# Attention's results stored in the projection's order from GpSimd's queue, and one block's mean and scale turned by TensorE

## The chip, the cores and the metric

The program runs on one core of a Trainium2 chip. The core has TensorE (PE in the profile: it multiplies matrices; PEld is its loading of weights), VectorE (DVE), ScalarE (ACT), GpSimd (POOL) and SyncE (SP), and 16 DMA engines that all queues share. Each engine works through its own instructions in order and waits for others through semaphores. A DMA is issued by an engine, in that engine's order, and lands later. The metric is device microseconds of one execution.

## The reference

A layer norm without weights, then two branches that read it, and their sum with the input:

```
xn  = layernorm(x)                       # x: 2048 rows of 576, fp32
qkv = xn @ wqkv                          # 32 heads of 18
out = x + attention(q, k, v) @ wo        # each row sees 8 keys: itself and every 2nd row behind it
        + relu(xn @ w1 + b1)**2 @ w2 + b2   # 576 -> 4608 -> 576
```

All is fp32.

## The kernel before

**Tiling.** The 2048 rows are 4 blocks b of 512, the heads 4 groups g of 8. The TensorE operands are split into a high and a low part in fp32r (ACT makes the high part by a copy, DVE the low part by a subtraction), and each product is made from high*high, high*low and low*high. Block 0 is normalised row by row and turned by TensorE (`open_rows`). Blocks 1 to 3 are loaded already turned (`load_xt`, features on the partitions), so mean and inverse standard deviation must lie along the free axis there: `statistics` computes them with rows on the partitions, a small tile `mr` of 128 x 8, line 146 stores it transposed into DRAM (`mr` too), and `load_mb` (line 161) loads it from there to all 128 partitions (`mb`). `normalize` needs `mb`.

**Attention.** `qkv_row` makes k, v and q of 128 rows (line 295), ACT puts them into the stage tile `st` (line 285), and line 288 stores them into DRAM (`kscr`, `vscr`, `qscr`). `fetch` loads them back per (b, g) with the rows behind (lines 315 and 317: `q`, and `kv` for k and for v; 3 `kv` buffers, 2 `q` buffers), so that DVE can work with 4 consecutive rows on each partition (`attention`, lines 333 to 371). The result replaces q and is stored whole by line 369 into DRAM (`o`, 512 rows of 144). The output projection wants other cuts of it: `regroup` (line 661) loads each block back in two parts, columns 0 to 95 into `st` (k = 0) and 96 to 143 into an `r4` buffer (k = 1), with 16 DMAs each (line 671), and DVE, ACT and DVE turn and split the five pieces (`o_hi`, `o_lo`; lines 683 and 684).

**Stages.** `open_rows`, then `q0` (the projection rows of blocks 0 and 1: `row(r)` for r = 0 to 27, with other work between them as `pieces` and attention's steps as `side`), `phase_a(0)` (the first layer of the FFN for blocks 0 and 1 in 18 pairs of feature tiles, with seven products in place of eight, and the second layer for block 0; block 1's activations `h` go to DRAM, line 539), `phase_b0` (the second layer of block 1 from the stored `h`, loaded by line 740, and the projection rows of blocks 2 and 3), `phase_a(1)` and `phase_b1` (the same for blocks 2 and 3). The output projection of a block (`o_ops`) comes at the end of its second layer.

**Order.** It is written out by hand for TensorE, ACT, DVE and SP, in the order in which the Python calls stand (`manual_schedule`). SP issues nearly all DMAs, in that order: if one waits for its data or its buffer, all behind it wait too, among them `w2r` (the second layer's weights, line 444, 3 buffers ahead), `w1r` (the first layer's, line 417) and `h`. GpSimd makes the power for the inverse standard deviation (line 129) and little else.

Of the kernel before, what the change touches and what calls it, by code (L numbers as in the profile page):

```python
# [25 lines left out]
G = 4  # L26
# [19 lines left out]
def block_kernel(ctx: ExitStack, tc: tile.TileContext, x, xt, wqkv, wo, w1, b1, w2, b2, out):  # L46
# [4 lines left out]
    ps = ctx.enter_context(tc.tile_pool(name="ps", bufs=1, space=bass.MemoryType.PSUM))  # L51
    dram = ctx.enter_context(tc.tile_pool(name="dram", bufs=1, space=bass.MemoryType.DRAM))

    ctx.enter_context(tc.manual_schedule(engines={ET.PE, ET.Activation, ET.DVE, ET.SP}))

    xv = x.rearrange("(b p j) d -> b p j d", p=P, j=NJ)
    ov = out[:DM].rearrange("(c p) (b t) -> b p c t", p=P, b=NB)
# [20 lines left out]
    b2t = const.tile([P, 64], F32, name="b2t")[:, :NC]  # L78

    scr = {k: [dram.tile([PAD + S, CG], F32, name=f"{k}scr{g}") for g in range(G)] for k in "kvq"}  # L80
    oscr = {(b, g): dram.tile([TB, CG], F32, name=f"o{b}{g}") for b in range(NB) for g in range(G)}
    mrscr = {b: dram.tile([2 * NJ, P], F32, name=f"mr{b}") for b in range(1, NB)}
    hscr = [[dram.tile([P, 4 * TB], F32, name=f"h{s}{p}") for p in range(NP)] for s in range(2)]

# [52 lines left out]
    def statistics(b):  # L137
        mr = sb.tile([P, 2, NJ], F32, name="mr")
        for j in range(NJ):
            for k in range(2):  # L140
                bn_stats(b, rows_of[b], j, k)
            mean_var(b, j)
            nc.vector.tensor_copy(mr[:, 0, j:j + 1], ln[b, j][:, 0:1])
            inverse_std(mr[:, 1, j:j + 1], ln[b, j][:, 1:2])
            if j == NJ - 1:
                nc.sync.dma_start(mrscr[b].rearrange("n p -> p n"), mr.rearrange("p k j -> p (k j)"))
                measured.add(b)
                release()
            yield

    def load_xt(b):
        xm[b] = sb.tile([P, NC - 1, TB], F32, name="w1r", bufs=2)
        nc.sync.dma_start(xm[b], xt[b, :, :NC - 1])
        xf[b] = {1: lambda: sb.tile([P, DE], F32, name="w2r", bufs=3)[:, :TB],
                 2: lambda: sb.tile([P, TB], F32, name="xf"), 3: lambda: four()[:, 0]}[b]()
        nc.sync.dma_start(xf[b], xt[b, :, NC - 1])

    def load_mb(b):
        assert b in measured
# [139 lines left out]
        a = t[:, j:j + 1, 0:1]  # L299
        return bass.AP(tensor=a.tensor, offset=a.offset, ap=[a.ap[0], [DIL * CG, W], *dims])  # L300

    loads, landed, queue, free = [], {}, [], [0]

    def fetch():
        while free[0] and loads:
            free[0] -= 1
            kind, b, g = loads.pop(0)
            if kind == "x":
                load_rows(b)
                landed["x", b] = True  # L310
                continue
            t = landed[kind, b, g] = sb.tile([P, NE, CG], F32, name="kv", bufs=3)
            if kind == "k":
                q = landed["q", b, g] = sb.tile([P, NJ, CG], F32, name="q", bufs=2)
                nc.sync.dma_start(q.rearrange("p j c -> p (j c)"),
                                  flat(scr["q"][g], (PAD + b * TB) * CG, [NJ * CG, P], NJ * CG))
            nc.sync.dma_start(t.rearrange("p e c -> p (e c)"),
                              flat(scr[kind][g], (PAD + b * TB - HALO) * CG, [NJ * CG, P], NE * CG))

    def release():  # L320
# [12 lines left out]
    def attention(b, g):  # L333
        k, q = landed.pop(("k", b, g)), landed.pop(("q", b, g))
        lg = sb.tile([P, NA, W], F32, name="lg")
        mx = sb.tile([P, NA], F32, name="mx")
        sm = sb.tile([P, NA], F32, name="sm")
        for j in range(NJ):
            pr = sb.tile([P, W, CG], F32, name="pr")
            tt(pr, q[:, j:j + 1].to_broadcast([P, W, CG]), shifted(k, j, [1, CG]), ALU.mult)  # L340
            if j == NJ - 1:
                release()
            yield
            nc.vector.tensor_reduce(out=lg[:, j * HG:(j + 1) * HG].rearrange("p a w -> p w a"),  # L344
                                    in_=pr.rearrange("p w (a d) -> p w a d", d=DH), axis=AX.X, op=ALU.add)
# [12 lines left out]
        v = landed.pop(("v", b, g))  # L358
        for j in range(NJ):
            pr = sb.tile([P, W, CG], F32, name="pr")  # L360
            at = lg[:, j * HG:(j + 1) * HG].rearrange("p a w -> p w a")
            tt(pr.rearrange("p w (a d) -> p w a d", d=DH), at[:, :, :, None].to_broadcast([P, W, HG, DH]),
               shifted(v, j, [DH, HG], [1, DH]), ALU.mult)
            yield
            tt(pr[:, :4], pr[:, :4], pr[:, 4:], ALU.add)
            tt(pr[:, :2], pr[:, :2], pr[:, 2:4], ALU.add)
            tt(q[:, j], pr[:, 0], pr[:, 1], ALU.add)
            if j == NJ - 1:
                nc.sync.dma_start(oscr[b, g].rearrange("(p j) c -> p j c", j=NJ), q)
                release()  # L370
            yield

# [240 lines left out]
    def phase_a(s, filler):  # L613
        b = 2 * s
        ffn_pair(s, 0, filler, first=True)
        open_y(b)
        for p in range(1, NP):
            h, ops = hs.pop(s * NP + p - 1), []

            def work(i):  # L620
                if i in (0, 2):
                    ops.extend(tile_products(b, 2 * p - 2 + i // 2, h))
                add(b, ops[7 * i:7 * i + 7])

# [24 lines left out]
        w2_lo()  # L649
        load_h(s, 2)  # L650
        o_hi(b, 4)
        o_lo(b, 4)
        for c in range(NC):
            w2_hi()
            add(b, o_ops(b, c), range(NC) if c == NC - 1 else ())
            w2_lo()
        finish(b)

    ob = {}

    def regroup(b, k):
        if k == 0:
            t = sb.tile([P, NJ * G, OA], F32, name="st")
        else:
            t = sb.tile([P, NJ * G, OB], F32, name="r4", bufs=4)
        ob[b, k] = t
        a, z = ((0, OA), (OA, CG))[k]
        for g in range(G):
            rows = oscr[b, g].rearrange("(i l j) c -> i l j c", i=G, j=NJ)
            for i in range(G):  # L670
                nc.sync.dma_start(t[g * L:(g + 1) * L].rearrange("l (j i) c -> l i j c", i=G)[:, i],  # L671
                                  rows[i, :, :, a:z])

    ot, of = {}, {}

# [379 lines left out]

    def q0():
        todo = [(b, g, j) for b, g in ((0, 1), (0, 3), (0, 2), (1, 3), (1, 2), (1, 1), (1, 0)) for j in range(NJ)]
        pieces = [statistics(1), once(load_mb, 1), split_wq(3, "S", lambda: load_wq(2)), normalize(1)]

        held = []  # L1060

        def row(r):
# [4 lines left out]
            if j == NJ - 1:  # L1067
# [2 lines left out]
                    if not b and g > 1:  # L1070
                        offer({3: 2, 2: 3}[g])

                if r < 5:
                    held.append(go)
                else:
                    go()

        for r in range(len(todo) - 2):
            row(r)
            if r == 5:  # L1080
                offer(0, 0)
                for late in held:
                    late()
                held.clear()
                pieces.insert(0, split_wq(2, "h", lambda: load_wq(0)))
            if r == 8:
                load_w1(0)
            if r == 11:
                run_all(pieces)
            if r == 15:  # L1090
# [1 line left out]
            if r == 19:  # L1092
                split_up.discard(0)
                pieces.insert(0, split_wq(0, "h"))
            if r == 23:
                run_all(pieces)
                combine_w1(0)
                load_w1(1)
                for n in range(3):
                    load_w2(n)  # L1100
            if r in (24, 25):
                w1_hi(0, r - 24)
                w1_lo(0, r - 24)
            else:
                run(pieces, 3 if r < 4 or 15 <= r < 20 else 2)

        def filler(i):
            if i < 2:
# [11 lines left out]
    nc.sync.dma_start(b1t, b1)  # L1120
    nc.sync.dma_start(b2t, b2)
    load_xt(1)
    with tc.manual_schedule(engines={ET.Pool}):
        open_rows()
    for g in range(1, G):
        for k in "kv":
            nc.sync.dma_start(scr[k][g][:PAD], zero)
# [57 lines left out]
```

## Time and profile before

| | us |
|---|---|
| median of 3 runs (lowest, highest) | 1218.41 (1218.04, 1218.84) |
| profiled execution, its own time | 1218.07 |
| its span | 1216.4 |
| PE busy | 1140.7 |
| DVE busy | 916.5 |
| ACT busy | 573.3 |
| POOL busy | 13.5 |

The span lacks 1.7 us of the execution's own time. PE's busy time leaves 75.7 us of the span; where these lie, and what ends them, is what the prediction reads. The stages in the span: `open_rows` to about 21 us, `q0` to 118, `phase_a(0)` to 477, `phase_b0` to 707, `phase_a(1)` to 1060, `phase_b1` to the end. In the rows shown, a line of the timeline is: start, duration, engine, line, operation, out<-in, count, and in brackets the engine's idle time before it and what ended that; "SPq" is SP issuing a DMA. A line of the waits is: who, for whom, total us, times, longest.

### The profile page before, as it was taken

What the parts mean: (1) busy time and instruction counts of PE and PEld (TensorE: products, weight loads), DVE (VectorE), ACT (ScalarE), POOL (GpSimd) and SP (SyncE); (2) the same over time, 40 slices, a digit from 0 to 9 for tenths busy, and PEclk for the clock granted to TensorE, in tenths of its full rate; (3) what the DMA queues carried; (4) which work ended last, traced back from release to release, by engine and by line L of the source; (5) the groups of instructions that cost most, each with busy time, mean ns of one, the idle gap of its engine ahead of it and who ended that gap; (6) DMA issues with size and microseconds to landing.
All of it is one profiled execution on the core that took longest, in us unless ns stands there. A gap on an engine that the chain in (4) does not pass through costs nothing.

```text
span 1216.4 us, 13713 instructions
## 1 busy us (share of the span) xinstructions
PE 1140.7 (94%) x5013; PEld 950.8 (78%) x5013; DVE 916.5 (75%) x1202; ACT 573.3 (47%) x800; POOL 13.5 (1%) x32
## 2 busy tenths in 40 slices
PE   9695999999999988999999699999999999799968
PEld 7694788888888876888888578888888888578747
DVE  6498588887887855888777577888878787499624
ACT  5323666666676642522232246766666675222121
POOL 3000000000000000000000000000000000000000
PEclk9898999999999998999999899999999999899979
DMA  7575437466466477988766575364545528678573
GB/s 257 178 252 187 160 122 256 147 150 241 156 143 255 121 262 255 348 281 308 268 221 203 142 236 200 107 233 156 200 161 197 202 91 274 229 277 311 200 263 111
DMA packets 107140, 254.25 MB, mean 209 GB/s; under 512 B 30016, under 2 KB 57408, under 8 KB 92480
## 3 DMA queue, kind: packets, MB, share of 16 engines
q1 hardware_dynamic: 106784, 253.00, 61.8%
q8 instruction: 39, 0.64, 0.2%
q10 hardware_dynamic: 288, 0.37, 0.1%
q14 instruction: 29, 0.24, 0.1%
HBM read 191.90 MB, written 61.43 MB: 208 GB/s over the span
## 4 chain that ended last, share of the span: by engine, by line
PE 75%; DMA 8%; DVE 8%; SPq 5%; issue 2%; ACT 2%; POOL 0%; DVEq 0%; ACTq 0%; POOLq 0%
PE p L481 31%; PE p L512 26%; PE p L295 12%; PE p L516 5%; SPq L671 4%; DMA h<-h 3%; DVE pr L93 3%; DVE w2s L93 2%; DMA w2r<-in_wo 1%; DMA w2r<-in_w 1%; DMA mr<-mr 1%; DMA qscr<-st 1%; ACT w2s L454 1%; PE p L973 1%; DVE w1r L93 1%
## 5 line engine op out<-in xcount | busy, mean ns | idle before, releaser
L481 PE MATMUL p<-h,w2s 128*128 128x512 f32 x2010 | 492.1, 393 | 16.7 <-DMA h<-h 13.6
L481 PEld LDWEIGHTS p<-h,w2s 128*128 128x128 f32 x2010 | 378.8, 189 | 102.3 <-issue 14.3
L512 PE MATMUL p<-X,w1s 128*128 128x512 f32 x864 | 221.4, 392 | 13.5 <-ACT w1s L427 11.8
L512 PEld LDWEIGHTS p<-X,w1s 128*128 128x128 f32 x864 | 162.5, 189 | 49.3 <-ACT w1s L427 12.2
L93 DVE TENSOR_TENSOR w2s<-w2r,w2s 128x576 fp32r<-128x576 f32 x164 | 123.4, 754 | 87.9 <-ACT w2s L454 86.4
L454 ACT ACTIVATE w2s<-w2r 128x640 fp32r<-128x640 f32 x164 | 119.8, 732 | 138.1 <-DMA w2r<-in_w 72.0
L512 PE MATMUL p<-S,w1s 128*128 128x512 f32 x648 | 165.5, 391 | 1.8 <-DVE r L93 1.8
L512 PEld LDWEIGHTS p<-S,w1s 128*128 128x128 f32 x648 | 122.1, 189 | 28.1 <-DVE r L93 2.7
L93 DVE TENSOR_TENSOR h<-r,h 128x1024 fp32r<-128x1024 f32 (+2 forms) x78 | 93.2, 1199 | 46.1 <-ACT r L527 45.4
L93 DVE TENSOR_TENSOR w1s<-w1r,w1s 128x1024 fp32r<-128x1024 f32 x72 | 88.2, 1225 | 28.7 <-ACT w1s L427 27.8
L519 ACT ACTIVATE r<-r,b1t 128x512 f32<-128x512 f32 x72 | 51.9, 721 | 116.7 <-DVE r L93 116.7
L285 ACT ACTIVATE st<-p 128x432 f32<-128x432 f32 x64 | 32.9, 528 | 156.7 <-PE p L295 92.4
L481 PE MATMUL p<-w1s,w2s 128*128 128x512 f32 x260 | 73.9, 450 | 27.4 <-ACT w2s L454 27.4
L93 DVE TENSOR_TENSOR pr<-q,kv 128x1152 f32<-128x1152 f32 x64 | 86.7, 1354 | 6.3 <-issue 5.5
L481 PEld LDWEIGHTS p<-w1s,w2s 128*128 128x128 f32 x260 | 57.7, 224 | 43.0 <-ACT w2s L454 29.8
L344 DVE TENSOR_REDUCE lg<-pr 128x64 f32<-128x1152 f32 x64 | 86.5, 1352 | 1.5
L93 DVE TENSOR_TENSOR pr<-lg,kv 128x1152 f32<-128x1152 f32 x64 | 86.7, 1354 | 1.0
L523 ACT ACTIVATE h<-r 128x1024 fp32r<-128x1024 f32 x72 | 76.1, 1057 | 9.2 <-DMA h<-h 8.1
L93 DVE TENSOR_TENSOR pr<-pr 128x576 f32<-128x576 f32 (+1 forms) x128 | 77.6, 607 | 3.4
L427 ACT ACTIVATE w1s<-w1r 128x1024 fp32r<-128x1024 f32 x72 | 75.7, 1051 | 2.0 <-PE p L481 1.9
L527 ACT ACTIVATE r<-r 128x1024 f32<-128x1024 f32 x72 | 76.0, 1055 | 1.2
L516 PE MATMUL p<-x,w1s 128*128 128x512 f32 x216 | 66.5, 389 | 0.0
(124 smaller groups left out, 964.5 us busy)
## 6 DMA issues: line engine op xcount, KB each, us to landing
h<-h SPq DMA_DIRECT2D x72, 1024.0 KB, 5.9
w2r<-in_w SPq DMA_DIRECT2D x144, 320.0 KB, 4.7
w1r<-in_w SPq DMA_DIRECT2D x36, 640.0 KB, 4.0
kv<-kscr SPq DMA_DIRECT2D x16, 1296.0 KB, 7.4
kv<-vscr SPq DMA_DIRECT2D x16, 1296.0 KB, 7.7
r<-in_wqkv SPq DMA_DIRECT2D x16, 432.0 KB, 6.2
w2r<-in_wo SPq DMA_DIRECT2D x20, 320.0 KB, 5.7
w1r<-in_xt SPq DMA_DIRECT2D x6, 1024.0 KB, 6.5
```

The lines of the kernel that those rows point to most:

```text
L93: return nc.vector.tensor_tensor(out=out, in0=a, in1=b, op=op)
L295: nc.tensor.matmul(p[:, :QW], l, r, start=k == 0, stop=k == len(mm) - 1)
L344: nc.vector.tensor_reduce(out=lg[:, j * HG:(j + 1) * HG].rearrange("p a w -> p w a"), in_=pr.rearrange("p w (a d) -> p w a d", d=DH), axis ...
L427: nc.scalar.activation(w1s[n, k][:, 0], raw1[n][:, 4 * k:4 * k + 4], AF.Copy)
L454: nc.scalar.activation(w2s[stream[i]][:, :DE], raw2[i], AF.Copy)
L481: nc.tensor.matmul(yp[b][c], v, a, start=c not in yb[b], stop=c in last and c not in [o[0] for o in ops[i + 1:]], skip_group_check=True)
L512: nc.tensor.matmul(to, l, r, start=start and i == 0, stop=i == len(mm) - 1, skip_group_check=True)
L516: nc.tensor.matmul(to, weight(LEFT, k, f), v, start=False, stop=k == 1, skip_group_check=True)
L519: nc.scalar.activation(to, a, AF.Relu, bias=b1t[:, f:f + 1])
L523: nc.scalar.activation(h[:, 0], r, AF.Square)
L527: nc.scalar.activation(r, r, AF.Square)
L671: nc.sync.dma_start(t[g * L:(g + 1) * L].rearrange("l (j i) c -> l i j c", i=G)[:, i], rows[i, :, :, a:z])
```

## The change

- `attention` stores its result from GpSimd's queue, cut into the projection's two parts and already in the projection's row order: 8 DMAs per (b, g) (4 per part) where there was one on SP. `regroup` is then one plain DMA per part, on GpSimd's queue too, in place of 16 on SP.
- From row 6 of `q0` on, the loads of q, k and v go through GpSimd's queue (`lane`). Those of (0, 0) and the q and k of (0, 1) stay on SP.
- Block 1's `mr` is turned by TensorE into PSUM, copied by ACT to an 8 x 128 tile, and stored by a plain DMA. Blocks 2 and 3 keep the transposing store.
- In `q0` the pieces stand in another order: the statistics and the splitting of group 3's weights are run to the end right behind row 2, and `load_mb(1)`, `load_wq(2)` and the first attention loads are issued there; `load_w1(0)` comes at row 5 (it was row 8), `load_w2` at row 21 (it was row 23).
- At the end of `phase_a`, the third load of `h` is issued behind the second output projection piece, not ahead of the first.
- GpSimd's instructions are now in hand-written order throughout.

```diff
-    ctx.enter_context(tc.manual_schedule(engines={ET.PE, ET.Activation, ET.DVE, ET.SP}))
+    ctx.enter_context(tc.manual_schedule(engines={ET.PE, ET.Activation, ET.DVE, ET.SP, ET.Pool}))
...
-    oscr = {(b, g): dram.tile([TB, CG], F32, name=f"o{b}{g}") for b in range(NB) for g in range(G)}
+    OPART = ((0, OA), (OA, CG))
+    oscr = {(b, k): dram.tile([P, NJ * G, z - a], F32, name=f"o{b}{k}") for b in range(NB) for k, (a, z) in enumerate(OPART)}
...
-                nc.sync.dma_start(mrscr[b].rearrange("n p -> p n"), mr.rearrange("p k j -> p (k j)"))
+                if b > 1:
+                    nc.sync.dma_start(mrscr[b].rearrange("n p -> p n"), mr.rearrange("p k j -> p (k j)"))
+                mrs[b] = mr
...
+    def turn_mr(b, i):
+        y = bank(i)
+        nc.tensor.transpose(y[:2 * NJ, :P], mrs[b].rearrange("p k j -> p (k j)"), ident)
+        t = sb.tile([2 * NJ, P], F32, name="mrt")
+        nc.scalar.activation(t, y[:2 * NJ, :P], AF.Copy)
+        nc.sync.dma_start(mrscr[b], t)
...
-                nc.sync.dma_start(q.rearrange("p j c -> p (j c)"),
+                lane[0].dma_start(q.rearrange("p j c -> p (j c)"),
                                   flat(scr["q"][g], (PAD + b * TB) * CG, [NJ * CG, P], NJ * CG))
-            nc.sync.dma_start(t.rearrange("p e c -> p (e c)"),
+            lane[0].dma_start(t.rearrange("p e c -> p (e c)"),
                               flat(scr[kind][g], (PAD + b * TB - HALO) * CG, [NJ * CG, P], NE * CG))
...
-                nc.sync.dma_start(oscr[b, g].rearrange("(p j) c -> p j c", j=NJ), q)
+                for k, (a, z) in enumerate(OPART):
+                    rows = oscr[b, k][g * L:(g + 1) * L].rearrange("l (j i) c -> l i j c", i=G)
+                    for i in range(G):
+                        nc.gpsimd.dma_start(rows[:, i], q[i * L:(i + 1) * L, :, a:z])
                 release()
...
-        load_h(s, 2)
         o_hi(b, 4)
         o_lo(b, 4)
         for c in range(NC):
             w2_hi()
             add(b, o_ops(b, c), range(NC) if c == NC - 1 else ())
             w2_lo()
+            if c == 1:
+                load_h(s, 2)
...
-        for g in range(G):
-            rows = oscr[b, g].rearrange("(i l j) c -> i l j c", i=G, j=NJ)
-            for i in range(G):
-                nc.sync.dma_start(t[g * L:(g + 1) * L].rearrange("l (j i) c -> l i j c", i=G)[:, i],
-                                  rows[i, :, :, a:z])
+        nc.gpsimd.dma_start(t.rearrange("p r c -> p (r c)"), oscr[b, k].rearrange("p r c -> p (r c)"))
...
-        pieces = [statistics(1), once(load_mb, 1), split_wq(3, "S", lambda: load_wq(2)), normalize(1)]
+        pieces = [statistics(1), split_wq(3, "S")]
...
-                if r < 5:
+                if r < 2:
...
-            if r == 5:
+            if r == 2:
+                run_all(pieces)
+                turn_mr(1, 7)
+                load_mb(1)
+                load_wq(2)
                 offer(0, 0)
                 for late in held:
                     late()
                 held.clear()
+                pieces += [normalize(1)]
+            if r == 5:
+                lane[0] = nc.gpsimd
+                load_w1(0)
                 pieces.insert(0, split_wq(2, "h", lambda: load_wq(0)))
-            if r == 8:
-                load_w1(0)
...
+            if r == 21:
+                run_all(pieces)
+                for n in range(3):
+                    load_w2(n)
             if r == 23:
-                run_all(pieces)
                 combine_w1(0)
                 load_w1(1)
-                for n in range(3):
-                    load_w2(n)
...
-            else:
-                run(pieces, 3 if r < 4 or 15 <= r < 20 else 2)
+            elif r != 3:
+                run(pieces, 3 if r < 2 or 15 <= r < 20 else 2)
```

More of the change, by code (lines that the diff above doesn't have):

```diff
@@ L300, in shifted @@
         return bass.AP(tensor=a.tensor, offset=a.offset, ap=[a.ap[0], [DIL * CG, W], *dims])
-    loads, landed, queue, free = [], {}, [], [0]
+    loads, landed, queue, free, lane = [], {}, [], [0], [nc.sync]
     def fetch():
@@ L666, in regroup @@
         ob[b, k] = t
-        a, z = ((0, OA), (OA, CG))[k]
-        for g in range(G):
-            rows = oscr[b, g].rearrange("(i l j) c -> i l j c", i=G, j=NJ)
-            for i in range(G):
-                nc.sync.dma_start(t[g * L:(g + 1) * L].rearrange("l (j i) c -> l i j c", i=G)[:, i],
-                                  rows[i, :, :, a:z])
+        nc.gpsimd.dma_start(t.rearrange("p r c -> p (r c)"), oscr[b, k].rearrange("p r c -> p (r c)"))
     ot, of = {}, {}
@@ L1122, in block_kernel @@
     load_xt(1)
-    with tc.manual_schedule(engines={ET.Pool}):
-        open_rows()
+    open_rows()
     for g in range(1, G):
```

## The prediction

> **What bounds the kernel now.** I read the page's busy times first, then what TensorE waited for, then the timeline around each wait.
>
> ```profile
> span 1216.4 us, 13713 instructions
> ...
> PE 1140.7 (94%) x5013; PEld 950.8 (78%) x5013; DVE 916.5 (75%) x1202; ACT 573.3 (47%) x800; POOL 13.5 (1%) x32
> ```
>
> ```profile
> PE p L481 <- ACT w2s L454: 29.7, 7, 7.9
> PE p L481 <- DMA h<-h: 13.6, 2, 11.4
> PE p L512 <- ACT w1s L427: 11.8, 1, 11.8
> PE p L295 <- ACT h L251: 9.3, 1, 9.3
> ```
>
> TensorE is the bound, but it idles 1216.4 - 1140.7 = 75.7 us, of which these eleven waits are 64.4. They are not spread over the stages: each is a few us long and lies at the start or at a block's end. So the change is worth what it takes from these places, and nothing in the long stretches between, where PE never stops.
>
> A long wait costs more than itself, since the matmuls behind it run slow:
>
> ```profile
> 118.13 3.33 PE L512 MATMUL p<-X,w1s 128*128 128x512 f32 x6 [11.85 <-ACT w1s L427]
> ...
> 126.54 1.54 PE L512 MATMUL p<-S,w1s 128*128 128x512 f32 x6
> ```
>
> ```profile
> 451.62 6.29 PE L481 MATMUL p<-w1s,w2s 128*128 128x512 f32 x14 [3.67 <-ACT w2s L454]
> ...
> 710.07 3.33 PE L481 MATMUL p<-w1s,w2s 128*128 128x512 f32 x14
> ```
>
> ```profile
> 1080.00:1100.00 20.00, 17.82 (x79) 14.47 (x78) 17.75 (x23) 4.29 (x7) 0.00 (x0) 1.00 0.86 336
> ```
>
> Six matmuls take 3.33 us behind the wait and 1.54 at full speed; fourteen take 6.29 and 3.33 (0.238 each). A wait of 3.67 us thus loses about 3 us more. The stretch from 1080 us holds 2.18 us of waiting and its granted clock stayed 1.00: short waits cost only themselves.
>
> **The start: mean and scale.**
>
> ```profile
> 29.34 0.75 SPq L146 DMA_DIRECT2D mr<-mr  x1
> ...
> 31.79 1.38 ACT L251 ACTIVATE S<-r 128x864 fp32r<-128x864 f32 x2 [1.17 <-DMA r<-in_wqkv]
> ...
> 39.36 0.33 SPq L161 DMA_DIRECT2D mb<-mr  x1
> ...
> 44.29 4.88 DVE L93 TENSOR_TENSOR w1r<-w1r,mb 128x1024 f32<-128x1024 f32 x4 [9.97 <-DMA mb<-mr]
> ...
> 52.87 5.06 PE L295 MATMUL p<-h,X 128*128 128x432 f32 x12 [9.33 <-ACT h L251]
> ```
>
> ```profile
> kscr<-pr SPq DMA_DIRECT2D x4, 9.0 KB, 1.6
> ```
>
> The transposing store takes 39.36 - 29.34 = 10.0 us, the load of `mb` 4.9 more; then DVE starts, then ACT, and PE has waited 9.33. The change adds a transpose (one matmul of PE, under 0.3 us), an ACT copy and a plain store of 4 KB. The nearest row for that store is the 9 KB one: 1.6 us. But the copy stands in ACT's queue behind the split of group 3, which ends at 31.79 + 1.38 = 33.2 since its weights come late, and behind row 2's copy: about 33.9. Store issued 34.3, landed 36, `mb` 40.9: 3.4 us earlier than 44.29, not 10. In the changed order ACT makes both halves of X (DVE's four operations, to 45.8, first), row 5's copy, then the first `h` piece: row 8 starts at 48.4, 4.5 us before 52.87. 4.7 us of the 9.3 stay.
>
> **The start: attention's transfers.**
>
> ```profile
> 61.65 1.36 DVE L93 TENSOR_TENSOR pr<-q,kv 128x1152 f32<-128x1152 f32 x1 [5.54 <-issue]
> ...
> 105.28 0.33 SPq L369 DMA_DIRECT2D o<-q  x1
> ...
> 110.73 1.60 DVE L93 TENSOR_TENSOR w1r<-w1r 128x512 f32<-128x512 f32 x3
> ...
> 116.60 0.53 ACT L285 ACTIVATE st<-p 128x432 f32<-128x432 f32 x1 [13.60 <-DMA qscr<-st]
> ```
>
> ```profile
> 524.40 5.49 PE p L295 x28
> ```
>
> At 105 us SP stood at `o<-q`, waiting for DVE; the stores of `st` behind it left late, ACT waited 13.60 us for the stage tile, and only then made `w1s`, for which PE waited 11.85. With stores and loads on GpSimd's queue that wait goes. Late next is DVE: the first FFN product needs `combine_w1` (110.73). DVE took 110.73 + 1.60 - 61.65 = 50.7 us from attention's first operation to its end; the changed order has one reduction, one product and one attention step of about 1.4 us less ahead of it, some 46.6 us are left. DVE normalises from 40.9, waits 2.5 us for ACT, and reaches attention at 55.5 (its data, issued near 38, is there). So `combine_w1` ends at 102.1, ACT's piece at 103.2. PE, from 48.4 with 18 rows of 2.75 us (the chain's row has two of them, 28 matmuls, in 5.49) and 2.5 lost to the clock, is ready at 100.4. Phase A starts at 103.2, not 118.13: 14.9 us. The wait left, 2.8 us, is between the 2.18 that cost no clock and the 3.67 that did; I count half of the 2.7 us that the clock lost here. **Start: 16.2 us.**
>
> **The price on GpSimd's queue.** This trace has no DMA issued by GpSimd. 128 stores, 43 loads and 8 regroup loads go there; SP loses 16 stores, 128 regroup loads and the same 43 loads. Nearest rows below: one SP issue is 0.33 us. From above: 17.42 us for the 16 of one regroup, 1.09 each with all waits. I take 1.09 per DMA, as the strided pieces are the same ones, and keep 0.33 and twice 1.09 as ends.
>
> ```profile
> 441.73 17.42 SPq L671 DMA_DIRECT2D r<-o  x16
> ...
> 447.76 1.06 ACT L523 ACTIVATE h<-r 128x1024 fp32r<-128x1024 f32 x1 [5.74 <-DMA h<-h]
> ...
> 462.88 14.24 PE L481 MATMUL p<-w1s,w2s 128*128 128x512 f32 x51 [4.97 <-ACT w2s L454]
> ```
>
> The Trainium skill's page "DMA: Bandwidth & Descriptors", section "Anatomy of one DMA — SWDGE (gpsimd) path", speaks against the change: every DMA from GpSimd has a fixed cost of about 2.0 us, most of it the wait for its landing, and small ones should be joined. If eight stores paid that one behind the other (an estimate from that figure: 16 us for a group in place of 8.7), the time would be near the price rival's 1187 in place of 1158; no row here shows which.
>
> **Block 0's end (441 to 477).** Two waits, 3.67 + 4.97, and the clock, 6.29 - 3.33 and 14.24 - 51 x 0.238: 13.7 us. The second was for `r<-o`. Now: eight stores from 427.5 (8.7 us), their landing (2.4), q, k and `r<-o` (3.3), landing 5: 447, before its use near 452. SP is free for `w2r` and `h`. What is late next is the `h` store: ACT's 5.74 us wait for it is only shortened. I leave 2 us twice. **9.7.**
>
> **Block 1's end (672 to 707).**
>
> ```profile
> 668.57 12.90 PE L481 MATMUL p<-h,w2s 128*128 128x512 f32 x56
> ...
> 672.42 11.23 SPq L671 DMA_DIRECT2D st<-o  x16
> ...
> 683.70 10.22 SPq L671 DMA_DIRECT2D r<-o  x16
> ...
> 688.26 5.78 PE L481 MATMUL p<-w1s,w2s 128*128 128x512 f32 x14 [6.79 <-ACT w2s L454]
> ...
> 698.16 9.12 PE L481 MATMUL p<-w1s,w2s 128*128 128x512 f32 x28 [4.12 <-ACT w2s L454]
> ```
>
> The plain load of `st` still waits for the last stage stores (issued to 670.8, about 3.7 us to land): issued near 674.5, landed 680.5, 3.5 us of turning and splitting, first product at 684 (PE is ready at 681.5), second at 689 in place of 698.16: 9.2 us, and 9.12 - 28 x 0.238 = 2.4 of the clock. **11.6.**
>
> **Block 2's end.**
>
> ```profile
> 1028.79 12.94 SPq L671 DMA_DIRECT2D r<-o  x16
> ...
> 1045.57 14.71 PE L481 MATMUL p<-w1s,w2s 128*128 128x512 f32 x51 [7.87 <-ACT w2s L454]
> ```
>
> Its results have been stored long before; the load stands on GpSimd's queue behind a v load of 1023 us, lands near 1030, and is wanted at 1035. 7.87 + 14.71 - 12.1: **10.5.**
>
> **Block 3's end.**
>
> ```profile
> 1113.65 0.33 SPq L369 DMA_DIRECT2D o<-q  x1
> ...
> 1144.41 0.33 SPq L369 DMA_DIRECT2D o<-q  x1
> 1144.79 11.10 SPq L671 DMA_DIRECT2D st<-o  x16
> ...
> 1165.42 12.43 PE L481 MATMUL p<-h,w2s 128*128 128x512 f32 x42 [11.39 <-DMA h<-h]
> ...
> 1179.89 11.42 PE L481 MATMUL p<-h,w2s 128*128 128x512 f32 x42 [2.04 <-ACT w2s L454]
> ```
>
> Two regroups held SP, and with it `h` and `w2r`: 11.39 + 2.04, and 2.4 + 1.4 of the clock, 17.2 us. At a price c per DMA the load lands at 1144.4 + 9c + 5; DVE has five weight tiles to split first and PE runs on them to 1160.5, so a stall of 9c - 8.9 is left: 0.9 at 1.09, nothing at 0.33, 10.7 at 2.18. **16.3.** The 2.18 us at 1092 stay.
>
> Between the ends nothing is gained or lost: a (b, g) costs GpSimd 11 DMAs, 12 us, and 10 of landing, in the 30.8 us that the fastest attention needs (1113.65 to 1144.41). `mr` of blocks 2 and 3 now queues behind DMAs on GpSimd; `mb` is wanted more than 70 us later. Moving `h`'s third load costs nothing: it lands 20 us before use.
>
> **The sum.** 16.2 + 9.7 + 11.6 + 10.5 + 16.3 = 64.3; I take off 4 us, since kv loads that leave on another queue now share the engines with `w2r` and `h` at each end: 60. The profiled execution took 1218.07, so 1158, and the same against the median, 1218.41, 0.3 above it.
>
> **Rivals.** *The price is double* (2.18): block 3's stall 10.7 in place of 0.9, block 0's about 5 more, and in the last stage 11 x 2.18 + 10 = 34 us do not fit 30.8, 3 us for each of three groups; with the clock lost again at two places (5), 29 us are given back: 1187. For it speaks that no row bounds GpSimd's issue from above; against it that GpSimd is otherwise idle.
>
> *The early part doesn't do what it says*: `mb` comes only 3.4 us earlier, and if the changed start only shifts DVE's wait for q, k and v (DMA is near its limit from 60 us on), the start gives 5: 1169.
>
> *GpSimd's DMAs hold up DVE*, and it gets slower.
>
> ```profile
> 9.00 0.60 DVE L907 TENSOR_TENSOR h<-w1r,h 128x432 fp32r<-128x432 f32 x1
> ...
> 11.81 1.12 POOL L907 TENSOR_TENSOR h<-w1r,h 128x432 fp32r<-128x432 f32 x1
> ...
> 12.48 0.92 DVE L907 TENSOR_TENSOR h<-w1r,h 128x432 fp32r<-128x432 f32 x1
> ```
>
> The same DVE operation took 0.60 us alone and 0.92 while GpSimd computed: 0.32 held. If writing a DMA's orders holds DVE likewise, for the 1.09 us of each, the 44 of the last stage (DVE busy 17.75 of 20) and some 25 of the start cost up to 75 us, more than the 60 won: 1233. It decides from about 0.9 us held per DMA; at 0.32 it costs 22, 1180. The Trainium skill, "SBUF — State Buffer", "Who interferes with whom", says that a DVE instruction with two SBUF inputs is held only by a GpSimd instruction that reads SBUF; the two rows agree, and by it writing orders would not hold DVE.
>
> **Chances.** My forecast (1142 to 1174) 0.70; double price 0.15; weak start 0.06 (its time falls into my range); slower 0.05; still more gained 0.04. The range reaches from 1140 (all 64.4 us of waits and half of some 19 of the clock) to 1193 (double price, a few us more). A difference under 0.2%, 2.4 us, couldn't be told from none. Faster 0.94, within 0.01, slower 0.05.
>
> **What would show it.** Right: no SP issue at `regroup` longer than 2 us; PE's waits for `w2s` and `h` at the four ends under 4 us each; first FFN product near 103 us; GpSimd's issues near 1 us. Wrong: GpSimd's queue solid for over 20 us per group, DVE operations longer than 1.36 us, or PE waiting at the ends on `st<-o` or `r<-o`.

## The result and the profile after

The changed kernel takes 1151.61 us (median of 4 runs, 1150.65 to 1152.73), beside 1218.22 us (1217.94 to 1218.84) of the kernel before on the same chip: 0.945 of it, with a 95% interval of 0.944 to 0.947. The prediction said 1158. The profiled execution took 1151.24 us, its span is 1149.3.

The page of the changed kernel, the busy times (part 1) and one of the costliest groups (part 5: busy us, mean ns of one, idle time ahead):

```profile
span 1149.3 us, 13816 instructions
...
PE 1122.4 (98%) x5014; PEld 939.7 (82%) x5014; DVE 914.7 (80%) x1202; ACT 572.5 (50%) x801; POOL 110.9 (10%) x211
...
L382 POOL DMA_DIRECT2D o<-q x128 | 69.2, 608 | 539.2 <-DVE q L94 537.6
```

PE idles 1149.3 - 1122.4 = 26.9 us where it was 75.7. That is 48.8 us of the 67.1; the other 18.3 are PE's busy time, 1140.7 - 1122.4, for the same matmuls (and one transpose): what had run at a reduced clock behind the long waits (the mean granted clock over the span was 0.967 and is 0.993). GpSimd's 128 stores take 69.2 us of its time, 0.54 each: one lasts 608 ns, but the next begins before it ends.

What PE waits for in the changed kernel (total us, times, longest):

```profile
PE p L494 <- ACT w2s L467: 5.3, 4, 2.3
PE p L525 <- ACT w1s L440: 3.9, 1, 3.9
...
PE p L305 <- ACT h L261: 2.6, 1, 2.6
PE p L525 <- DVE w1s L94: 2.4, 1, 2.4
...
PE p L494 <- DMA h<-h: 1.5, 1, 1.5
```

Line 494 is the second layer and the output projection (481 before), 525 the first layer (512), 305 the projection rows (295). Of 29.7 us for `w2s` 5.3 are left, of 13.6 for `h` 1.5, of 11.8 for `w1s` 3.9, of 9.3 at row 8 2.6.

To see where the time went, I cut the span at four matmuls that both kernels have: the one behind a wait of 0.9 us in the first FFN pairs (twice, once in each `phase_a`), and the first tile of `phase_b0` and of `phase_b1`. In PE's timeline of the kernel before:

```profile
141.29 1.65 PE L512 MATMUL p<-S,w1s 128*128 128x512 f32 x6 [0.90 <-DVE r L93]
...
476.95 3.41 PE L481 MATMUL p<-h,w2s 128*128 128x512 f32 x13
...
727.91 1.67 PE L512 MATMUL p<-S,w1s 128*128 128x512 f32 x6 [0.92 <-DVE r L93]
...
1060.11 4.09 PE L481 MATMUL p<-h,w2s 128*128 128x512 f32 x16
```

and of the changed kernel:

```profile
127.73 1.65 PE L525 MATMUL p<-S,w1s 128*128 128x512 f32 x6 [0.92 <-DVE r L94]
...
448.95 13.15 PE L494 MATMUL p<-h,w2s 128*128 128x512 f32 x56
...
689.06 1.65 PE L525 MATMUL p<-S,w1s 128*128 128x512 f32 x6 [0.92 <-DVE r L94]
...
1010.27 44.88 PE L494 MATMUL p<-h,w2s 128*128 128x512 f32 x196
```

The differences between neighbouring cuts give the table, with the same four rows read in every experiment (us of span in each part):

| kernel | start | to block 0's end | block 1's end | block 2's end | block 3's end | span |
|---|---|---|---|---|---|---|
| before | 141.3 | 335.7 | 251.0 | 332.2 | 156.3 | 1216.4 |
| changed | 127.7 | 321.2 | 240.1 | 321.2 | 139.0 | 1149.3 |
| gain (predicted) | 13.6 (16.2) | 14.4 (9.7) | 10.9 (11.6) | 11.0 (10.5) | 17.3 (16.3) | 67.1 (60) |
| e1_sp_queue | 128.4 | 323.4 | 238.8 | 321.2 | 152.0 | 1163.9 |
| e2_old_layout | 128.8 | 322.7 | 251.6 | 332.3 | 148.2 | 1183.6 |
| e3_loads_sp | 127.8 | 327.3 | 241.5 | 321.2 | 146.1 | 1164.0 |
| e4_old_start | 139.3 | 321.2 | 239.8 | 321.2 | 139.4 | 1160.9 |
| e5_start_alone | 127.0 | 336.0 | 253.0 | 330.7 | 158.0 | 1204.7 |
| e6_no_turn | 134.3 | 321.2 | 240.3 | 321.2 | 139.8 | 1156.8 |
| e7_double | 128.5 | 322.7 | 241.1 | 321.2 | 144.2 | 1157.7 |
| e8_w1_early | 118.3 | 321.4 | 244.9 | 321.2 | 143.5 | 1149.3 |
| e9_steps_back | 119.7 | 321.6 | 240.3 | 321.2 | 139.9 | 1142.6 |
| e10_turn_dve | 117.1 | 321.7 | 240.6 | 321.2 | 140.5 | 1141.1 |
| e11_more | 118.3 | 322.0 | 236.8 | 321.2 | 136.2 | 1134.5 |

Block 2's part is 321.2 us in every kernel that has no stall there: PE never stops in it, so its length is that of its matmuls. Starts of the same code differ by about a microsecond between runs.

### The profile page after: what moved, and what is told of

Its sections match the earlier page's. It is cut to its first block, busy times and chain, and to the rows that moved or that the text cites. A ratio compares the mean times of both kernels' runs of the same rounds, so it can differ in the third digit from the quotient of the medians.

```text
span 1149.3 us, 13816 instructions
## 1 busy us (share of the span) xinstructions
PE 1122.4 (98%) x5014; PEld 939.7 (82%) x5014; DVE 914.7 (80%) x1202; ACT 572.5 (50%) x801; POOL 110.9 (10%) x211
## 4 chain that ended last, share of the span: by engine, by line
PE 79%; DVE 12%; DMA 4%; issue 3%; ACT 1%; POOL 0%; DVEq 0%; ACTq 0%; POOLq 0%; SPq 0%
PE p L494 35%; PE p L525 29%; PE p L305 9%; PE p L529 5%; DVE pr L94 5%; DVE w2s L94 2%; DVE w1r L94 1%; DMA h<-in_xt 1%; DMA r<-in_wqkv 1%; DMA st<-o 1%; PE p L982 1%; DMA o<-q 1%; DVE w1s L94 1%; DVE r L94 0%; ACT w2s L467 0%
## 5 line engine op out<-in xcount | busy, mean ns | idle before, releaser
L494 PE MATMUL p<-h,w2s 128*128 128x512 f32 x2010 | 487.0, 390 | 4.8 <-ACT w2s L467 2.6
L382 POOL DMA_DIRECT2D o<-q x128 | 69.2, 608 | 539.2 <-DVE q L94 537.6
L94 DVE TENSOR_TENSOR pr<-lg,kv 128x1152 f32<-128x1152 f32 x64 | 86.7, 1354 | 1.1
L94 DVE TENSOR_TENSOR pr<-q,kv 128x1152 f32<-128x1152 f32 x64 | 86.6, 1354 | 0.9
L494 PE MATMUL p<-w1s,w2s 128*128 128x512 f32 x260 | 62.3, 398 | 2.9 <-ACT w2s L467 2.7
```

Source lines behind the costliest of these rows:

```text
L94: return nc.vector.tensor_tensor(out=out, in0=a, in1=b, op=op)
L382: nc.gpsimd.dma_start(rows[:, i], q[i * L:(i + 1) * L, :, a:z])
L494: nc.tensor.matmul(yp[b][c], v, a, start=c not in yb[b], stop=c in last and c not in [o[0] for o in ops[i + 1:]], skip_group_check=True)
```

## The experiments

### Queue or layout?

**All of it on SP again, the new layout kept.**

```diff
-                        nc.gpsimd.dma_start(rows[:, i], q[i * L:(i + 1) * L, :, a:z])
+                        nc.sync.dma_start(rows[:, i], q[i * L:(i + 1) * L, :, a:z])
...
-        nc.gpsimd.dma_start(t.rearrange("p r c -> p (r c)"), oscr[b, k].rearrange("p r c -> p (r c)"))
+        nc.sync.dma_start(t.rearrange("p r c -> p (r c)"), oscr[b, k].rearrange("p r c -> p (r c)"))
...
-                lane[0] = nc.gpsimd
```

> The changed kernel, but the stores of attention's results, the two regroup loads and all loads of q, k and v are issued by SP again; the new layout of the results, the start's order and the turned mean stay. My theory (SP's order is the cause: whatever stands behind a store or load that waits for DVE or for a landing leaves late): w2r, h and the stage stores are held up again at the start and at the ends of blocks 1 and 3, 1170 to 1195 us, with waits of PE for w2s over 4 us. Rival (the layout is the cause: 2 regroup DMAs in place of 32 and no small pieces): 1149 to 1156 us, since SP keeps only 10 short DMAs more per group.

Measured: 1166.35 us, 0.956 of before (0.954 to 0.957). That is between the two, and the table says why: start, block 1 and block 2 keep all of the gain, block 0 all but 2.2 us, and only block 3's end loses 13.0, so the whole lies below the range that I expected. There the SP timeline and PE's two long waits show the old stall:

```profile
1050.30 29.99 PE L494 MATMUL p<-h,w2s 128*128 128x512 f32 x124 [6.25 <-DMA h<-h]
...
1100.90 5.62 SPq L382 DMA_DIRECT2D o<-q  x8
...
1118.06 12.29 PE L494 MATMUL p<-h,w2s 128*128 128x512 f32 x45 [7.54 <-DMA h<-h]
```

SP stands at `o<-q` until 1100.9 and takes 5.6 us to issue the eight stores, and the `h` loads behind them come late. So SP's order is the cause at block 3's end, as the first theory had it; at the start and at blocks 1 and 2 it is not.

**The old layout, from GpSimd's queue.**

```diff
-                for k, (a, z) in enumerate(OPART):
...
-                        nc.gpsimd.dma_start(rows[:, i], q[i * L:(i + 1) * L, :, a:z])
+                nc.gpsimd.dma_start(oscr[b, g].rearrange("(p j) c -> p j c", j=NJ), q)
...
-        nc.gpsimd.dma_start(t.rearrange("p r c -> p (r c)"), oscr[b, k].rearrange("p r c -> p (r c)"))
+        a, z = ((0, OA), (OA, CG))[k]
+        for g in range(G):
+            rows = oscr[b, g].rearrange("(i l j) c -> i l j c", i=G, j=NJ)
+            for i in range(G):
+                nc.gpsimd.dma_start(t[g * L:(g + 1) * L].rearrange("l (j i) c -> l i j c", i=G)[:, i],
+                                    rows[i, :, :, a:z])
```

> The changed kernel, but attention's result is stored whole by one DMA and regroup loads with 16 DMAs per part, as before the change, both from GpSimd's queue. At 0.54 us per DMA a part takes 8.7 us to issue. My theory (the queue is most of it; the layout is worth something only where a regroup is followed closely by its use): block 1's end loses 8.1 us and 1 to 3 of clock, block 3's end 8.1 less 3.8 for the stores saved and 1 to 3 of clock, blocks 0 and 2 nothing: 1164 to 1172 us. Rival (the layout is most of it): over 1185 us. Rival (it makes no difference once the queue is free): 1150 to 1156 us.

Measured: 1183.79 us, 0.969 (0.967 to 0.972): 29 us of the gain are gone (34 in the profiled execution, which the table has; the four runs lie between 1178.92 and 1187.03), more than the queue theory allowed and close to the rival that the layout is most of it. Blocks 1 and 2 are back at the times of before (251.6 and 332.3), block 3 loses 9.2, block 0 only 1.5. GpSimd's and PE's timeline at block 1's end, and PE's at block 2's:

```profile
648.51 4.50 POOL L681 DMA_DIRECT2D st<-o  x8 [17.95 <-ACT w2s L463]
654.50 2.17 POOL L681 DMA_DIRECT2D st<-o  x4 [1.49 <-DMA st<-o]
...
662.06 8.66 POOL L681 DMA_DIRECT2D r<-o  x16
...
666.45 5.59 PE L490 MATMUL p<-w1s,w2s 128*128 128x512 f32 x14 [9.40 <-ACT w2s L463]
...
1021.63 13.90 PE L490 MATMUL p<-w1s,w2s 128*128 128x512 f32 x51 [8.76 <-ACT w2s L463]
```

Sixteen issues are 8.7 us where nothing holds them, as in the second part here. The first part took 13.6 us (648.51 to 662.06): after eight, GpSimd waits for earlier ones to land. The list of compiled instructions shows where this comes from. The DMAs of a kind of queue take turns on eight semaphores, so each waits for the one eight before it (here the kernel with doubled stores, below):

```
L383 DMACopy o_101<-q 64x1x96 [waits DMASW0_49]
L383 DMACopy o_102<-q 64x1x48 [waits DMASW1_49]
L383 DMACopy o_102<-q 64x1x48 [waits DMASW2_49]
```

and SP's regroup in the kernel before:

```
L671 DMACopy st<-o_102 32x4x96 [waits DMAHW2_49]
L671 DMACopy st<-o_102 32x4x96 [waits DMAHW3_49]
L671 DMACopy st<-o_102 32x4x96 [waits DMAHW4_49]
```

Its 1.09 us per DMA were thus only in part a price of issuing: in the trace of before one issue of line 671 lasts 597 ns at the median, and the rest of the 17.42 us for sixteen is waiting for landings. The same DMAs from GpSimd last 548 ns here.

**The loads of q, k and v on SP.**

```diff
-                lane[0] = nc.gpsimd
```

> The changed kernel, but the loads of q, k and v stay on SP throughout; stores and regroup on GpSimd's queue. My theory (every DMA that waits for DVE holds what stands behind it on SP): a load waits for its buffer, that is for DVE's last read, and for the landing of GpSimd's stores where it takes q's buffer, so SP is held about as long as by the store before: 1160 to 1175 us. Rival (only the store and the 16-fold regroup held SP): 1149 to 1155 us.

Measured: 1164.63 us, 0.954 (0.953 to 0.955), in the range of the first theory: block 0's end loses 6.1 us, block 3's 7.1, the rest little. SP's waits for attention's results show how. In e1 it stood at their store:

```profile
SPq L382 <- DVE q L94: 102.2, 16, 13.4
```

and here it stands at the load of q into the same buffer (14.4 us in e1):

```profile
SPq L325 <- DMA o<-q: 131.0, 27, 15.6
```

With the stores on GpSimd's queue, a load of q on SP waits until they have landed, and so takes over the wait for DVE. The loads alone on SP thus cost about as much as everything on SP (1164.63 and 1166.35 us): with the new layout the queue helps only if both leave SP. Why block 0's end loses more here than in e1 (2.2) is not resolved. No run separates the later third load of `h`, or GpSimd's hand-written order, from the rest.

### The start

**The old order and the transposing store, with GpSimd's queue.** The body of `q0` is that of before, with this line, and `statistics` stores `mr` transposed for block 1 too:

```diff
             if r == 5:
                 offer(0, 0)
                 for late in held:
                     late()
                 held.clear()
+                lane[0] = nc.gpsimd
                 pieces.insert(0, split_wq(2, "h", lambda: load_wq(0)))
```

> The changed kernel, but with the start's order of before and the transposing store of block 1's mean and scale; GpSimd's queue takes stores, regroup and the loads from row 6 on. My theory: row 8's first matmul is back near 52.9 us; the first product of the FFN comes when DVE is through, about 50.7 us after attention's first operation at 61.7 us, so near 113.5 us (102.4 changed, 118.1 before): 1160 to 1166 us. Rival (the start's gain came from the queue alone): 1150 to 1154 us. Rival (it came from the order alone): 1165 us and more.

**The start's order and the turn alone**, everything else as before (GpSimd's instructions stay in hand-written order):

```diff
-                nc.sync.dma_start(mrscr[b].rearrange("n p -> p n"), mr.rearrange("p k j -> p (k j)"))
+                if b > 1:
+                    nc.sync.dma_start(mrscr[b].rearrange("n p -> p n"), mr.rearrange("p k j -> p (k j)"))
+                mrs[b] = mr
...
+                turn_mr(1, 7)
+                load_mb(1)
```

> The kernel before, with only the start's part of the change: the new order of the pieces in q0 and the turned mean and scale of block 1; all DMAs on SP, old layout. My theory: row 8 starts near 46.7 us; at phase A's start SP still stands at the store of attention's first result, ACT still waits for the stage tile, but all of it some 6 to 10 us earlier: first FFN product at 108 to 112 us, 1208 to 1213 us, and together with the run of the old start the two gains add up to the whole of 66.6 us within 4. Rival (the start's order needs GpSimd's queue): 1214 us and more.

Measured: e4 1165.99 us, 0.955 (0.953 to 0.957); e5 1204.52 us, 0.987 (0.984 to 0.990). In e4 only the start is longer, by 11.6 us; in e5 only the start is shorter, by 14.3, a bit more than the whole change has there, and more than I expected (1208 to 1213 us). The two parts add up: 1216.4 - 1160.9 = 55.5 and 1216.4 - 1204.7 = 11.7 make 67.2, the whole 67.1. That they meet so closely is luck: by the medians, each against its own runs of before, they are 54.6 and 15.0, 69.6 beside 66.6. So the queue is worth about 2 us at the start with the old order (141.3 to 139.3) and nothing with the new one (127.0 and 127.7), and the order nearly all. In e4's timelines of ACT and PE:

```profile
106.17 0.53 ACT L294 ACTIVATE st<-p 128x432 f32<-128x432 f32 x1 [2.09 <-DMA qscr<-st]
112.98 1.06 ACT L439 ACTIVATE w1s<-w1r 128x1024 fp32r<-128x1024 f32 x1 [6.28 <-DVE w1r L94]
...
114.09 1.22 PE L524 MATMUL p<-X,w1s 128*128 128x512 f32 x2 [6.74 <-ACT w1s L439]
```

GpSimd's queue does take ACT's wait for the stage tile away, from 13.60 us to 2.09. But then ACT waits for DVE's `w1r`, and the first product comes only 4.0 us earlier than at 118.13. In e5's timelines of DVE and SP:

```profile
53.39 1.36 DVE L93 TENSOR_TENSOR pr<-q,kv 128x1152 f32<-128x1152 f32 x1
...
98.54 0.33 SPq L378 DMA_DIRECT2D o<-q  x1
...
101.53 0.38 SPq L297 DMA_DIRECT2D kscr<-st  x1
```

Attention begins at 53.4 where it began at 61.65, the store `o<-q` leaves at 98.5 where it left at 105.3, still on SP, and ACT no longer waits for the stage tile, with one group of stage stores behind `o<-q` where the trace of before has two.

**The turn alone undone**, in the changed order:

```diff
-                if b > 1:
-                    nc.sync.dma_start(mrscr[b].rearrange("n p -> p n"), mr.rearrange("p k j -> p (k j)"))
+                nc.sync.dma_start(mrscr[b].rearrange("n p -> p n"), mr.rearrange("p k j -> p (k j)"))
...
-                turn_mr(1, 7)
```

> The changed kernel, but block 1's mean and scale go out by the transposing store, in the changed order. My theory: the store takes 10 us in place of about 5.3 from the statistics' end through transpose, copy and store, but is issued near 29 us, not 33.9: mb lands near 43.5, not 39.4, row 8 starts 3 to 4 us later, and of this 3 to 5 us stay at the end: 1154 to 1157 us. Rival (what is lost at row 8 is caught up in the later wait for w1s): 1150 to 1153 us.

Measured: 1160.73 us, 0.952 (0.948 to 0.955); the start is 6.6 us longer, more than I expected. SP's timeline without the turn:

```profile
29.72 0.83 SPq L147 DMA_DIRECT2D mr<-mr  x1
40.83 0.33 SPq L170 DMA_DIRECT2D mb<-mr  x1
```

and with it, in the changed kernel:

```profile
33.88 0.34 SPq L166 DMA_DIRECT2D mr<-mrt  x1
35.15 0.34 SPq L171 DMA_DIRECT2D mb<-mr  x1
```

Each second line waits for the first to land: 11.1 us transposing, 1.3 plain, for the same 4 KB. None of the 5.7 us between 40.8 and 35.15 is hidden.

### The price on GpSimd's queue

Each store cut in two:

```diff
-                        nc.gpsimd.dma_start(rows[:, i], q[i * L:(i + 1) * L, :, a:z])
+                        for lo, hi in ((0, L // 2), (L // 2, L)):
+                            nc.gpsimd.dma_start(rows[lo:hi, i], q[i * L + lo:i * L + hi, :, a:z])
```

> The changed kernel with each of attention's stores cut into two: 16 DMAs per group on GpSimd's queue in place of 8, same bytes, same descriptors in all. My theory (what counts is the time to issue, 0.54 us each, and only at block 3's end is it uncovered): 4.3 us more at block 3's end and 1 to 3 of clock, elsewhere nothing: 1156 to 1160 us. Rival (the issue costs by descriptors, so half-size DMAs cost half): 1150 to 1153 us. Rival (each DMA has a fixed cost of about 2 us behind the others): over 1180 us.

Measured: 1158.82 us, 0.949 (0.947 to 0.952). Block 3's end is 5.2 us longer, the other places 0 to 1.5. GpSimd's and PE's timeline there, in the changed kernel:

```profile
1093.47 3.23 POOL L382 DMA_DIRECT2D o<-q  x6 [26.64 <-DVE q L94]
1096.87 1.06 POOL L382 DMA_DIRECT2D o<-q  x2 [0.17 <-issue]
1102.25 0.56 POOL L681 DMA_DIRECT2D st<-o  x1 [4.32 <-DMA o<-q]
...
1111.41 12.99 PE L494 MATMUL p<-h,w2s 128*128 128x512 f32 x56 [2.27 <-ACT w2s L467]
```

and with doubled stores:

```profile
1096.53 4.02 POOL L383 DMA_DIRECT2D o<-q  x8 [21.73 <-DVE q L94]
1101.45 0.51 POOL L383 DMA_DIRECT2D o<-q  x1 [0.90 <-DMA o<-q]
...
1104.88 3.02 POOL L383 DMA_DIRECT2D o<-q  x6 [2.00 <-DMA o<-q]
1107.86 0.59 POOL L682 DMA_DIRECT2D st<-o  x1
...
1117.72 15.02 PE L495 MATMUL p<-h,w2s 128*128 128x512 f32 x56 [5.51 <-ACT w2s L468]
```

A half-size DMA costs 0.50 us to issue where the whole cost 0.54, so the rival by descriptors falls; the fixed 2 us in a row fall too. The wait grows from 2.27 to 5.51, and the 56 matmuls behind it from 12.99 to 15.02: together 5.3 us.

### What bounds the changed kernel

**The first weights earlier.** The two waits left at phase A's start (3.86 and 2.43) come from attention steps ahead of the weights in DVE's order.

```diff
             if r == 21:
                 run_all(pieces)
                 for n in range(3):
                     load_w2(n)
-            if r == 23:
                 combine_w1(0)
                 load_w1(1)
-            if r in (24, 25):
-                w1_hi(0, r - 24)
-                w1_lo(0, r - 24)
-            elif r != 3:
+            if r in (23, 24):
+                w1_hi(0, r - 23)
+                w1_lo(0, r - 23)
+            elif r not in (3, 21, 22):
```

> The changed kernel with the first FFN weights made earlier: combine_w1(0) at row 21 in place of 23, the halves split at rows 23 and 24, and attention's steps of rows 21 and 22 left for later. My theory (the waits of 3.86 and 2.43 us at phase A's start are DVE's queue of attention steps ahead of the weights): both go, with about 2.4 us of clock: 1143 to 1147 us. Rival (DVE's steps only move and hold up PE in the first pair): 1149 to 1154 us.

Measured: 1151.69 us, 0.944 (0.941 to 0.946), no different from the changed kernel and in the rival's range, but not for the rival's reason: both waits went, and the start is 9.4 us shorter. What came back are 4.8 us at block 1's end and 4.4 at block 3's. DVE's last attention step in the changed kernel, and then in this one, with the window of the last stage (busy us of PE, PEld, DVE, ACT, POOL, then clock, DMA share, GB/s):

```profile
1092.87 0.31 DVE L94 TENSOR_TENSOR q<-pr 128x144 f32<-128x144 f32 x1
```

```profile
1093.77 0.31 DVE L94 TENSOR_TENSOR q<-pr 128x144 f32<-128x144 f32 x1
...
1005.00:1090.00 85.00, 82.83 (x359) 66.29 (x357) 81.75 (x107) 20.08 (x29) 10.82 (x20) 1.00 0.85 316
```

Everything began earlier, and attention still ended 0.9 us later: DVE is busy 81.75 of 85 us in the last stage. It was as full in the changed kernel (81.56 of the 85 us from 1010), so the steps that were put off at the start found no room there.

**The same, with the steps put back where DVE has time.**

```diff
             ffn_pair(s, p, work)
+            if s == 0 and p < 5:
+                side(1, False)
```

> The kernel of the earlier first weights (e8: its start was 9.4 us earlier, its end the same), with the four attention steps that it had left for later put back one by one behind pairs 1 to 4 of phase A, where DVE has idle time. My theory (in e8 DVE's chain of attention steps set the end of the last stage: DVE was busy 81.75 of 85 us there, and what is put off at the start is paid at blocks 1's and 3's ends): the waits of 6.3 us for w2s and 6.1 us for DVE's w2s go back to about 2 each, and the 9.4 us of the start stay: 1141 to 1145 us. Rival (the end is set by something else, such as the transfers of h and w2r): 1149 to 1153 us. Rival (the steps hold up PE in phase A instead): 1146 to 1150 us.

Measured: 1144.3 us, 0.937 (0.935 to 0.940). Blocks 1 and 3 are back at 240.3 and 139.9, and 8.1 us of the start stay. One attention step in each of four pairs decides it, so DVE's steps were what set the end; how they reach block 1's end in e8 (there the load of `st<-o` itself came late) is not resolved step by step.

**The turned tile copied by DVE**, ahead of the low parts of group 3's weights:

```diff
-        nc.scalar.activation(t, y[:2 * NJ, :P], AF.Copy)
+        nc.vector.tensor_copy(t, y[:2 * NJ, :P])
...
+            if r == 1:
+                run_all(pieces)
+                open_wq(3, "S")
+                wq_hi(3, 0), wq_hi(3, 1)
             if r == 2:
-                run_all(pieces)
                 turn_mr(1, 7)
                 load_mb(1)
+                wq_lo(3, 0)
...
```

> e9 with the turned mean and scale copied out of PSUM by DVE, which is idle then, ahead of the low parts of group 3's weights, in place of ACT behind their high parts. My theory (in the changed kernel the copy stood behind the split in ACT's queue from 30.4 to 33.6 us): the store is issued near 31 us in place of 33.9, mb lands near 36.5 in place of 39.4, PE's 2.6 us wait at row 8 goes, and as DVE is 3 us earlier at attention too, 2.5 to 3 us less than e9. Rival (row 8 is hidden by a later wait): the same as e9 within 1 us.

Measured: 1142.59 us, 0.936 (0.934 to 0.938). The store is issued at 30.3, as expected, but lands 3.5 us later, not 1.3 (`mb` issued at 33.8), and `mb` is there at 38.3, 1.1 earlier. Row 8's wait is 1.9 us. Against e9 the gain can't be told from none.

**More steps in the second `phase_a`, and the projection rows of blocks 2 and 3 a tile earlier.**

```diff
-            if s == 0 and p < 5:
+            if p < (5, 7)[s]:
...
-            while r < 32 and 32 * (n - 6) > 25 * r:
+            while r < 32 and 32 * (n - 6) > 24 * r:
...
-            if n == 31:
+            if n == 30:
```

> e10 with two more shifts of the same kind: six attention steps of blocks 2 and 3 behind pairs 1 to 6 of the second phase A, and the projection rows of blocks 2 and 3 a tile earlier, with the regroup of block 1 at tile 30 in place of 31. My theory: 8 us of DVE's steps taken from the last stage remove its wait of about 2 us, and the load of st<-o comes 6 us earlier against the wait of 2.15 us at block 1's end: 2 to 5 us less than e10. Rival (DVE then holds up PE's pairs, at 83 percent busy there): as much more as e10 or slower.

Measured: 1135.56 us, 0.931 (0.929 to 0.933), better than both kernels and 7.0 us less than e10, more than expected. Block 1's part is 3.8 us shorter and block 3's 4.3. Its span is 1134.5 us; from its page:

```profile
PE 1117.8 (99%) x5014; PEld 937.5 (83%) x5014; DVE 913.4 (81%) x1203; ACT 572.6 (50%) x800; POOL 111.1 (10%) x211
```

PE idles 16.7 us, and none of its waits at the blocks' ends is over 0.8.

## Why the prediction was right, and where it was not

**The bound.** Right: the whole gain lies at the start and the four ends, none between. The five terms make 64.3 us, the span lost 67.1. That they meet within 3 us is partly luck: the start gave 2.6 less than its term and block 0's end 4.7 more.

**The start: 13.6 for 16.2.** The steps of `mr` were right in kind: `mb` landed at 39.4 (40.9 said), row 8 ran at 46.7 (48.4). The first product came at 102.4 (103.2). PE's timeline of the changed kernel:

```profile
46.69 0.66 PE L305 MATMUL p<-h,X 128*128 128x432 f32 x2 [2.57 <-ACT h L261]
...
102.44 0.73 PE L525 MATMUL p<-X,w1s 128*128 128x512 f32 x2 [3.86 <-ACT w1s L440]
105.61 2.08 PE L525 MATMUL p<-X,w1s 128*128 128x512 f32 x4 [2.43 <-DVE w1s L94]
...
107.90 2.49 PE L525 MATMUL p<-S,w1s 128*128 128x512 f32 x6
```

The step that failed stands behind it. I followed ACT's high part of the weights and not DVE's low part, which the third matmul needs: it came 3.2 us after the first, behind two of attention's operations. With 2.43 us more to wait the clock was lost as before; I had counted half of it. The sentence "With stores and loads on GpSimd's queue that wait goes" is true but carries little of the gain: e4 has the wait nearly gone by that queue and gains 2.0 us at the start, since DVE is late next, as I had it; e5 has it gone with SP's queue. The order did it.

**The price c.** Wrong by a factor of two: 0.54 us, not 1.09. I had taken the 16 SP loads of one regroup with all their waits as the nearest row; the issue of one, 0.60 us in the same trace, was nearer. On the Trainium skill's page "DMA: Bandwidth & Descriptors", section "Anatomy of one DMA — SWDGE (gpsimd) path", I had read the fixed 2.0 us as a possible price behind one another: eight stores leave in 4.3 us and the last lands 4.3 us later, so here it is a latency that overlaps, which agrees with the page's own remark that it is mostly the wait for the landing. Its size does not agree: these stores took 4.1 us at the median (1.8 to 6.8) from issue to landing.

**Block 0's end: 14.4 for 9.7.** I left 2 us at each of two waits for ACT's wait for the `h` store; the changed kernel has no wait over 0.3 us there. With SP free the store leaves earlier, at 415.5 us; in e3, where SP holds the loads of q, k and v, it leaves at 423.4, and ACT waits 3.96 us for it.

**Blocks 1 and 2: 10.9 and 11.0 for 11.6 and 10.5.** Right, by the steps named: one plain load in place of 16 (e2, with the 16 back, loses 11.5 and 11.1 us there). In GpSimd's and DVE's timelines of the changed kernel, at block 1's and at block 3's end:

```profile
645.51 0.53 POOL L681 DMA_DIRECT2D st<-o  x1 [18.48 <-ACT w2s L467]
...
653.00 1.31 DVE L692 STREAM_TRANSPOSE r<-st 128x512 f32<-128x512 f32 x2 [3.77 <-DMA st<-o]
...
1109.36 0.71 DVE L692 STREAM_TRANSPOSE r<-st 128x512 f32<-128x512 f32 x1 [4.62 <-DMA st<-o]
```

At block 1 the load takes 7.5 us from issue to DVE's first turn, for the 6 assumed, and PE waits 2.15 us there.

**Block 3's end: 17.3 for 16.3**, by errors that nearly cancel. Nine DMAs took 4.9 us, not 9.8; the landing I had put at 5 us, but the stores must land before the load starts, 4.3 us, and the load takes 6.6 (1102.8 to 1109.4). From DVE's last step to the data are 16 us against 14.8, so PE waited 2.27 us where I had 0.9. At that length the clock held. That more was gained all the same comes for the most part from two other places: PE's busy time in this part fell from 136.4 to 131.4 us, 5.0 of clock where I had 3.8, and the wait of 2.18 us for `h` that I had let stay is 1.49.

**The 4 us for shared DMA engines**: not to be seen. They were set against no row, and without them the sum is 64.3.

**The rivals.** GpSimd's DMAs do not hold DVE. The product of q and k is an operation that runs beside them: in the changed kernel, seventeen of its 64 lie for more than 0.3 us beside GpSimd's issues. All 64, before and changed:

```profile
L93 DVE TENSOR_TENSOR pr<-q,kv 128x1152 f32<-128x1152 f32 x64 | 86.7, 1354 | 6.3 <-issue 5.5
```

```profile
L94 DVE TENSOR_TENSOR pr<-q,kv 128x1152 f32<-128x1152 f32 x64 | 86.6, 1354 | 0.9
```

and one of the seventeen, with the stores that it ran beside:

```profile
658.18 4.33 POOL L382 DMA_DIRECT2D o<-q  x8 [11.61 <-DVE q L94]
...
661.11 1.35 DVE L94 TENSOR_TENSOR pr<-q,kv 128x1152 f32<-128x1152 f32 x1
```

They last 1354 ns in both, and none of the seventeen is over 1.36 us. On the Trainium skill's page "SBUF — State Buffer", "Who interferes with whom", an operation with two SBUF inputs is held only by a GpSimd instruction that reads SBUF; the trace agrees, as far as issuing DMAs held none of these. The double price fell with c, and the weak start (5 us) with the 13.6 measured.

## What to carry to other kernels

Read the pace of a run of DMAs only after asking what each of them waits for: a row of issues can be paced by landings, and then its time is not all price; the duration of one issue is in the trace too. Where TensorE is the bound, cut the span at the same few matmuls in every kernel; a change's parts then add up place by place, and one can see which part did what. A stall removed by putting off work of another engine is paid at the next place where that engine is full; put the work where it has time, and the gain stays.

## What the runs showed of the hardware that was not expected

- A DMA issued by GpSimd costs 0.54 us when it moves 128 pieces and 0.50 when it moves half of them; up to eight were in flight without a wait. SP is not quicker with such strided pieces: for the 128 loads of the old `regroup`, 597 ns at the median from SP and 548 from GpSimd.
- Stored transposed, 4 KB in 4-byte pieces took 10.0 and 11.1 us to land; stored plain, 1.3 and 3.5.
- A wait of PE of 2.27 us cost no clock (56 matmuls in 12.99 us), one of 5.51 cost 2.0 us more (15.02), and two of 3.86 and 2.43 us close together about as much: 2.08 + 2.49 us for ten matmuls that take 2.6 at full speed (1.54 for six).
